# Converting weights with clamp, shift and mask, and two feed-forward chunks in halves, in a fused attention and feed-forward kernel

## The chip, the core and the metric

The kernel runs on one core of a Trainium2 chip. A core has a matrix engine (TensorE, PE in the profile), a vector engine (VectorE, DVE), a scalar engine (ScalarE, ACT), a general engine (GpSimd, POOL) and a queue that starts transfers (SyncE, SP). Each engine works through its own instructions in order and waits for others by semaphores. Matmuls write to PSUM, all else lives in SBUF. The metric is device time in microseconds (us) of one execution.

## What is computed

```python
def _attn_ref(q, k, v, w_phi):                  # q, k, v: 8 x 8 heads x 576 x 64
    def phi(x):
        proj = np.einsum('bhsd,df->bhsf', x, w_phi)                 # 64 -> 128
        proj = proj - np.max(np.abs(proj), axis=-1, keepdims=True)
        return np.concatenate([np.exp(proj), np.exp(-proj)], axis=-1)
    q_p, k_p = (phi(q), phi(k))
    kv = np.einsum('bhsf,bhsd->bhfd', k_p, v)
    z = np.sum(k_p, axis=2)
    num = np.einsum('bhsf,bhfd->bhsd', q_p, kv)
    den = np.einsum('bhsf,bhf->bhs', q_p, z)[..., None] + 1e-06
    return (num / den).astype(np.float32)

def _moe_ref(x, w_in, w_out):                   # x: 4608 x 512, w_in: 512 x 2048
    h = x @ w_in
    sp = np.where(h > 20.0, h, np.log1p(np.exp(np.minimum(h, 20.0))))
    g = h * np.tanh(sp)                         # Mish
    return (g @ w_out).astype(np.float32)       # w_out: 2048 x 512
```

The attention's output, 4608 tokens of 512 features, is the feed-forward's `x`. The attention's inputs are fp32, but `w_in` and `w_out` arrive as fp64; the kernel sees each element as two 32-bit words.

## The kernel before

**Attention.** The keys are cut into 36 key units of 512 columns (two heads). A unit is loaded (`k_load`, tile `kraw`), projected on PE (`k_proj`, `pp_k`, L122), its absolute maxima are taken on DVE (L127) and subtracted (L128), ACT makes two exponentials (`k_exp`), and PE adds keys times values into `kvps` (`k_sum`, L137); DVE copies each finished head pair to `kv` (L182). Values come by `v_load`, with `v` triple-buffered. The 4608 queries go in 18 chunks of 256 tokens with two query units each, (chunk, 0) and (chunk, 1): projection `pp_q`, maxima, subtraction to `e_q`, transposes to `dt` (L200), exponentials (L202), `num` on PE, a division on DVE (L217 to L219), and transposes to `xt`. ACT and DVE then split the result into `xTh` and `xTl`, two parts that together hold its fp32 precision. Queries of one batch need its `kv`, and so 4.5 key units.

**Feed-forward.** Each chunk runs through 16 tiles f of 128 hidden features. `ff_in` is 12 matmuls to `h` (L249, three products of the high and low parts by four weight pieces); `mish` takes two tiles at a time, Mish on ACT (L257) with a table of its own, and `gh` and `gl` as the two parts (L261, L262); `ff_out` is six matmuls of 512 columns (L276) into two `o` accumulators, which stay in PSUM for all 16 tiles of a chunk.

**Weights.** They are 32 pieces of 128 x 512: `in` (i, j), four row blocks i by four column blocks j, and `out` i, 16 row blocks. Tile f of `h` needs `in` (0 to 3, f // 4), and step f of `o` needs `out` f. The order is `in` j=0, then `out` 0-3, `in` j=1, `out` 4-7, `in` j=2, `out` 8-11, `in` j=3, `out` 12-15. `load_weight` fetches one piece (512 KB), `split_weight` (L81 to L101) turns the words into fp32 with a low remainder: DVE takes mantissa and exponent (L88, L89), ACT converts both to floats (L91, L92), DVE adds the low word (L93) and the sign (L94), POOL multiplies (L96), ACT rounds to the high part (L100), POOL subtracts for the low part (L101). The tile `w` shares three buffers with Mish's `u`.

**Order.** Every step is put at a time in a list (`at`), whose unit is one feed-forward tile: tile n of the 288 stands at n. From time -2 on a key and a query unit stand at every eighth unit; ahead of that, seven key units from -18.8 on lie 2.4 apart (`USTART`), the last two with the first two query units. The 32 pieces' conversions are spread evenly from -16.8 to 9, each loaded 3 ahead. The list is emitted in order of time, and the framework's scheduler then moves instructions a little by its own timeline. What stands on an engine is in fixed order.

Of the kernel before, what the change touches and what calls it, by code (L numbers as in the profile page):

```python
# [39 lines left out]
def attention_then_mish(ctx, tc, qT, kT, va, w_phi, w_in, w_out, out):  # L40
    nc = tc.nc

    const = ctx.enter_context(tc.tile_pool(name="const", bufs=1))
# [10 lines left out]
    one = const.tile([P, 1], F32, tag="one", name="one")
    nc.vector.memset(one, 1.0)
    exp_bias = const.tile([P, 1], F32, tag="exp_bias", name="exp_bias")
    nc.vector.memset(exp_bias, -7.0 * 2 ** 30)
# [23 lines left out]
    def split_weight(kind, i, j):  # L81

        nm = f"{kind}_{i}_{j}"
        words = weight[kind, i, j]
# [2 lines left out]
        scale = work.tile([P, 512], U32, tag="half", name=f"scale_{nm}", bufs=NHALF)
        nc.vector.tensor_scalar(w, high, 0xFFFFF, None, op0=ALU.bitwise_and)  # L88
        nc.vector.tensor_scalar(scale, high, 1, 21, op0=ALU.logical_shift_left, op1=ALU.logical_shift_right)  # L89

        nc.scalar.activation(w.bitcast(F32), w, AF.Identity, scale=2.0 ** -20, bias=one)  # L91
# [1 line left out]
        nc.vector.scalar_tensor_tensor(w.bitcast(F32), low, 2.0 ** -52, w.bitcast(F32), op0=ALU.mult, op1=ALU.add)  # L93
        nc.vector.scalar_tensor_tensor(scale, high, 0x80000000, scale, op0=ALU.bitwise_and, op1=ALU.bitwise_or)  # L94
# [1 line left out]
        nc.gpsimd.tensor_tensor(w, w, scale.bitcast(F32), op=ALU.mult)  # L96
# [3 lines left out]
        nc.scalar.copy(hi, w)  # L100
        nc.gpsimd.tensor_sub(lo, w, hi.bitcast(F32))  # L101
# [134 lines left out]

    def ff_in(c, f):
        nonlocal starting
# [24 lines left out]
            g_live[c, 2 * fp + f] = (gh, gl)  # L263

    def ff_out(c, f):
        if f == 0:
            o_live[c] = [ps_o.tile([P, DM], F32, tag="o", name=f"o_{c}_{tt}") for tt in range(2)]
        if f == NFT - 2:
            return
        for tt, ps in enumerate(o_live[c]):  # L270
            cols = slice(tt * P, (tt + 1) * P)
            for i in (f - 1, f) if f == NFT - 1 else (f,):
                gh, gl = g_live[c, i]
                wh, wl = weight["out", i, 0]
                for k, (g, w) in enumerate(((gh, wh), (gh, wl), (gl, wh))):
                    nc.tensor.matmul(ps, g[:, cols], w, start=(i == 0 and k == 0), stop=(i == NFT - 1 and k == 2))  # L276
            if f == NFT - 1:
                o = work.tile([P, DM], F32, tag="half", name=f"osb_{c}_{tt}", bufs=NHALF)
                if c == NCH - 1 and tt:
                    nc.vector.tensor_copy(o, ps)  # L280
                else:
                    nc.scalar.copy(o, ps)
                nc.sync.dma_start(out[c * CH + tt * P:c * CH + (tt + 1) * P, :], o)


    events = []
# [5 lines left out]
    steps = [(n - LEAD, n if n < NK else None, divmod(n - LEAD, 2) if 0 <= n - LEAD < 2 * NCH else None)
             for n in range(LEAD + 2 * NCH)]
    when = {n: 8.0 * n - 18.0 if n >= 2 else 8.0 * 2 - 18.0 - USTART * (2 - n) for n in range(-LEAD, 2 * NCH + 1)}
    for n, key, query in steps:
        t, t1 = when[n], when[n + 1]
# [19 lines left out]
    t0 = when[-LEAD]  # L316
    for i, pc in enumerate(pieces):
        when = t0 + W0 + (W1 - W0 - t0) * i / 31
        at(when - WLOAD, load_weight, *pc)
        at(when, split_weight, *pc)  # L320
# [41 lines left out]
```

## Time and profile before

| what | us |
|---|---|
| median of 3 runs (1248.95 to 1250.86) | 1249.59 |
| the profiled execution | 1249.79 |
| its span in the profile | 1247.8 |
| PE busy in the span | 1174.2 (94%) |
| ACT busy | 616.0 (49%) |
| DVE busy | 499.2 (40%) |
| POOL busy (all of it ahead of 185 us) | 91.0 (7%) |

The span is that of one execution taken by the profiler; the execution's own time is 2.0 longer. The page's columns "busy" count time with an instruction in progress, waiting for a port within an instruction included. A PE share of 94% says nothing by itself on where the other 6% lie, nor at which clock PE ran; the slices and stretches of the prediction do.

### The profile page before, as it was taken

Reading aid. Unit: us, or ns where it says so; the run is one execution under the profiler, and the core shown is the slowest. Engines: PE = TensorE matmul, PEld = TensorE weight load, DVE = VectorE, ACT = ScalarE, POOL = GpSimd, SP = SyncE. Lnnn points to the kernel's source line nnn. Section 1 sums busy time; section 2 is a strip of 40 time slices with the busy share of each in tenths; the row PEclk is TensorE's granted clock in tenths of the full one; section 3 lists DMA queues with packets and bytes.
Section 4 is the critical chain, followed back from the end, with each engine's and each line's share of the span. In section 5 each row is a group of like instructions: output and inputs, shape, how many; then the busy total and the mean of one; then the engine's idle time right before and its main releaser. Section 6 shows DMA issues by size and latency. Waiting matters only on the chain.

```text
span 1247.8 us, 26586 instructions
## 1 busy us (share of the span) xinstructions
PE 1174.2 (94%) x11632; PEld 1050.6 (84%) x11632; DVE 499.2 (40%) x991; ACT 616.0 (49%) x1023; POOL 91.0 (7%) x70
## 2 busy tenths in 40 slices
PE   5436899999999999999999999999999999999998
PEld 4426788888889888888898989888888889999997
DVE  7997783333333333333333333333333332222221
ACT  5544676454545454545445445444444445545421
POOL 3663350000000000000000000000000000000000
PEclk9567889999999999999999999999999999999999
DMA  9811101011111111011111111111011100000000
GB/s 354 329 28 44 34 9 46 19 46 29 46 29 37 38 29 46 18 46 29 46 29 46 29 46 29 35 29 46 29 46 29 35 18 27 1 18 10 10 18 17
DMA packets 25027, 57.67 MB, mean 46 GB/s; under 512 B 2768, under 2 KB 2896, under 8 KB 24912
## 3 DMA queue, kind: packets, MB, share of 16 engines
q1 hardware_dynamic: 24912, 55.98, 13.7%
q8 instruction: 91, 1.49, 0.5%
q14 instruction: 24, 0.20, 0.0%
HBM read 46.53 MB, written 9.44 MB: 45 GB/s over the span
## 4 chain that ended last, share of the span: by engine, by line
PE 89%; DVE 7%; ACT 1%; issue 1%; DMA 0%; POOL 0%; SPq 0%; DVEq 0%; ACTq 0%; POOLq 0%
PE o L276 33%; PE h L249 33%; PE kvps L137 5%; PE pp_q L122 5%; PE num L137 5%; PE pp_k L122 3%; PE dt L200 2%; PE xt L227 1%; DVE scale_in L94 1%; DVE w_in L93 1%; DVE scale_in L89 1%; DVE scale_out L89 1%; DVE w_out L93 1%; DVE m_k L127 1%; DVE w_in L88 1%
## 5 line engine op out<-in xcount | busy, mean ns | idle before, releaser
L249 PE MATMUL h<-xTh,win 128*128 128x256 f32 x2304 | 454.0, 282 | 1.5 <-DVE e_q L128 1.5
L249 PEld LDWEIGHTS h<-xTh,win 128*128 128x128 f32 x2304 | 370.9, 188 | 17.4 <-issue 1.7
L276 PE MATMUL o<-wout,gh 128*128 128x512 f32 x1152 | 380.1, 409 | 2.2 <-DVE kv L182 2.2
L262 DVE TENSOR_TENSOR gl<-u,gh 128x256 fp32r<-128x256 f32 x288 | 118.4, 439 | 548.6 <-ACT gh L261 546.2
L257 ACT ACTIVATE u<-h 128x512 f32<-128x512 f32 x144 | 86.1, 598 | 499.3 <-PE h L249 495.0
L249 PE MATMUL h<-xTl,win 128*128 128x256 f32 x1152 | 324.6, 282 | 0.0
L276 PE MATMUL o<-wout,gl 128*128 128x512 f32 x576 | 228.4, 397 | 0.0
L249 PEld LDWEIGHTS h<-xTl,win 128*128 128x128 f32 x1152 | 216.8, 188 | 12.1
L276 PEld LDWEIGHTS o<-wout,gh 128*128 128x128 f32 x1152 | 197.1, 190 | 34.8 <-DVE kv L182 2.4
L276 PEld LDWEIGHTS o<-wout,gl 128*128 128x128 f32 x576 | 108.9, 189 | 25.9 <-issue 0.2
L261 ACT CAST gh<-u 128x256 fp32r<-128x256 f32 x288 | 110.9, 409 | 38.7 <-PE o L276 19.6
L122 PE MATMUL pp_k<-w_phi,kraw 64*128 64x128 f32 x576 | 64.6, 315 | 32.8 <-issue 16.3
L122 PEld LDWEIGHTS pp_k<-w_phi,kraw 64*128 64x128 f32 x576 | 52.8, 212 | 50.7 <-issue 49.4
L137 PE MATMUL kvps<-v,e_k 128*64 128x66 f32 x2560 | 91.0, 233 | 1.6 <-ACT e_k L166 1.6
L137 PEld LDWEIGHTS kvps<-v,e_k 128*64 128x64 f32 x2560 | 85.1, 146 | 7.4 <-ACT e_k L166 2.3
L257 ACT ACT_TABLE_LOAD x68 | 87.2, 1283 | 1.2
L202 ACT ACTIVATE e_q<-dt 128x512 f32<-128x512 f32 x144 | 78.2, 595 | 17.0 <-PE dt L200 16.5
L202 ACT ACT_TABLE_LOAD x67 | 86.0, 1283 | 1.0
L137 PE MATMUL num<-kv,e_q 128*64 128x66 f32 x2304 | 77.3, 224 | 6.7 <-ACT e_q L202 5.0
L122 PE MATMUL pp_q<-w_phi,qraw 64*128 64x128 f32 x576 | 74.3, 293 | 7.1 <-issue 3.9
L137 PEld LDWEIGHTS num<-kv,e_q 128*64 128x64 f32 x2304 | 73.1, 140 | 8.6 <-ACT e_q L202 5.2
L122 PEld LDWEIGHTS pp_q<-w_phi,qraw 64*128 64x128 f32 x576 | 62.1, 195 | 16.8 <-issue 14.1
(45 smaller groups left out, 809.4 us busy)
## 6 DMA issues: line engine op xcount, KB each, us to landing
v<-va SPq DMA_DIRECT2D x32, 330.0 KB, 3.0
...
```

Of the source, the lines that this page charges most:

```text
L88: nc.vector.tensor_scalar(w, high, 0xFFFFF, None, op0=ALU.bitwise_and)
L89: nc.vector.tensor_scalar(scale, high, 1, 21, op0=ALU.logical_shift_left, op1=ALU.logical_shift_right)
L93: nc.vector.scalar_tensor_tensor(w.bitcast(F32), low, 2.0 ** -52, w.bitcast(F32), op0=ALU.mult, op1=ALU.add)
L122: nc.tensor.matmul(ps[j][:, n], raw[rows, n * P:(n + 1) * P], w_phi2[rows], start=True, stop=True)
L137: nc.tensor.matmul(ps[rows], lhsT[:, rows], rhs[h], start=start, stop=stop, skip_group_check=True)
L200: nc.tensor.transpose(ps[:, n * P:(n + 1) * P], e[:, 0, n * P:(n + 1) * P], ident)
L202: table(nc.scalar.activation(e[:, s, :], ps, AF.Exp, scale=2.0 * s - 1.0))
L249: nc.tensor.matmul(ps, w[:, wcol], x[:, cc % 2, :], start=(n == 0), stop=(n == 11))
L257: table(nc.scalar.activation(u, hv, AF.Mish))
L261: nc.scalar.copy(gh, u[:, f * CH:(f + 1) * CH])
L262: nc.vector.tensor_sub(gl, u[:, f * CH:(f + 1) * CH], gh.bitcast(F32))
L276: nc.tensor.matmul(ps, g[:, cols], w, start=(i == 0 and k == 0), stop=(i == NFT - 1 and k == 2))
```

## The change

**Conversion.** One ACT instruction (Abs) copies the high words, which lie at every second place, to a packed tile. DVE clamps them as floats, shifts them left by 3 under a mask, and puts sign and top bit back; that is the fp32 value. A mask keeps sign and exponent (`t`), and `low * 2^-52 * t` is what the low word adds. ACT rounds to the high part, POOL subtracts and adds. So per piece ACT has two instructions where it had three, DVE five where it had four, and POOL two as before.

**Feed-forward order.** The first two chunks (`NHALVED`) go through tiles 0-7 of chunk 0, 0-7 of chunk 1, 8-15 of chunk 0, 8-15 of chunk 1. The first half's `o` is copied to `part` in SBUF by ACT, and DVE adds it to the second half's.

**Time table.** Five key units lead, then four query units, then four key units (`FIRST_STEPS`); from time 14 on the steps are as before. Conversions stand at `WTIMES` (12 pieces ahead of -2 to 2, the last at 22), loads at a line of their own from -19 on, 0.6 apart. `v` has two buffers where it had three.

```diff
+SMALL, LARGE = 2.0 ** -15, 1.875 * 2.0 ** 16 - 2.0 ** -7
-NRAW, NE, NV, NKV = 4, 6, 3, 10
+NRAW, NE, NV, NKV = 4, 6, 2, 10
+FIRST_STEPS = ((-16.0, 0, None), (-14.0, 1, None), (-12.0, 2, None), (-10.0, 3, None), (-8.0, 4, None), (-6.0, None, 0),
...
-W0, W1 = 2.0, 9.0
+NHALVED = 2
+WL0, WL1 = -19.0, 0.6
+WTIMES = [t0 + (t1 - t0) * i / 4 for t0, t1 in ((-14, -7), (-7, -2), (-2, 2), (2, 6), (6, 10), (10, 14), (14, 18), (18, 22))
+          for i in range(4)]
...
-        nc.vector.tensor_scalar(w, high, 0xFFFFF, None, op0=ALU.bitwise_and)
-        nc.vector.tensor_scalar(scale, high, 1, 21, op0=ALU.logical_shift_left, op1=ALU.logical_shift_right)
-        nc.scalar.activation(w.bitcast(F32), w, AF.Identity, scale=2.0 ** -20, bias=one)
-        nc.scalar.activation(scale, scale, AF.Relu, scale=2.0 ** 23, bias=exp_bias)
-        nc.vector.scalar_tensor_tensor(w.bitcast(F32), low, 2.0 ** -52, w.bitcast(F32), op0=ALU.mult, op1=ALU.add)
-        nc.vector.scalar_tensor_tensor(scale, high, 0x80000000, scale, op0=ALU.bitwise_and, op1=ALU.bitwise_or)
+        nc.scalar.activation(w.bitcast(F32), high.bitcast(F32), AF.Abs)
+        nc.vector.tensor_scalar(w.bitcast(F32), w.bitcast(F32), SMALL, LARGE, op0=ALU.max, op1=ALU.min)
+        nc.vector.tensor_scalar(w, w, 3, 0x3FFFFFF8, op0=ALU.logical_shift_left, op1=ALU.bitwise_and)
+        nc.vector.scalar_tensor_tensor(w, high, 0xC0000000, w, op0=ALU.bitwise_and, op1=ALU.bitwise_or)
+        nc.vector.tensor_scalar(t.bitcast(U32), w, 0xFF800000, None, op0=ALU.bitwise_and)
+        nc.vector.scalar_tensor_tensor(t, low, 2.0 ** -52, t, op0=ALU.mult, op1=ALU.mult)
         w = w.bitcast(F32)
-        nc.gpsimd.tensor_tensor(w, w, scale.bitcast(F32), op=ALU.mult)
         nc.scalar.copy(hi, w)
-        nc.gpsimd.tensor_sub(lo, w, hi.bitcast(F32))
+        nc.gpsimd.tensor_sub(w, w, hi.bitcast(F32))
+        nc.gpsimd.tensor_tensor(lo, w, t, op=ALU.add)
...
+            if f < NFT - 1:
+                part_live[c, tt] = work.tile([P, DM], F32, tag="part", name=f"part_{c}_{tt}", bufs=2 * NHALVED)
+                nc.scalar.copy(part_live[c, tt], ps)
+                continue
+            if parts == 2:
+                nc.vector.tensor_tensor(o, ps, part_live.pop((c, tt)), op=ALU.add)
...
+    tiles = [(c, half * NFT // 2 + f) for half in range(2) for c in range(NHALVED) for f in range(NFT // 2)]
+    tiles += [(c, f) for c in range(NHALVED, NCH) for f in range(NFT)]
     for n in range(total):
-        c, f = divmod(n, NFT)
+        c, f = tiles[n]
```

Two places show how the instructions move. The first is DVE, where the first query unit's subtraction `e0_q_0_0` stands; names carry the piece or unit and end in a buffer number. Before:

```order
L88 TENSOR_SCALAR w_out_8_0_1034<-words_out_8_0_858 128x512
L93 SCALAR_TENSOR_TENSOR w_in_3_2_1011<-words_in_3_2_826,w_in_3_2_1011 128x512
L89 TENSOR_SCALAR scale_out_8_0_1035<-words_out_8_0_858 128x512
L128 TENSOR_TENSOR e0_q_0_0_630<-pp0_q_0_0_620,m0_q_0_0_631 128x512
L93 SCALAR_TENSOR_TENSOR w_out_8_0_1034<-words_out_8_0_858,w_out_8_0_1034 128x512
L128 TENSOR_TENSOR e1_q_0_0_634<-pp1_q_0_0_621,m1_q_0_0_635 128x512
L94 SCALAR_TENSOR_TENSOR scale_out_8_0_1035<-words_out_8_0_858,scale_out_8_0_1035 128x512
```

And now:

```order
L94 TENSOR_SCALAR w_in_3_1_819<-w_in_3_1_819 128x512
L98 SCALAR_TENSOR_TENSOR t_in_2_1_786<-words_in_2_1_202,t_in_2_1_786 128x512
L95 SCALAR_TENSOR_TENSOR w_in_3_1_819<-words_in_3_1_206,w_in_3_1_819 128x512
L97 TENSOR_SCALAR t_in_3_1_820<-w_in_3_1_819 128x512
L98 SCALAR_TENSOR_TENSOR t_in_3_1_820<-words_in_3_1_206,t_in_3_1_820 128x512
L132 TENSOR_TENSOR e0_q_0_0_520<-pp0_q_0_0_510,m0_q_0_0_521 128x512
L132 TENSOR_TENSOR e1_q_0_0_524<-pp1_q_0_0_511,m1_q_0_0_525 128x512
L186 COPY kv_2_424<-kvps_2_339 128x264
L186 COPY kv_3_491<-kvps_3_426 128x264
L131 TENSOR_REDUCE m0_q_0_1_628<-pp0_q_0_1_617 128x4
```

The subtraction stood among pieces `in` (3, 2) and `out` 8, the 20th and 21st; now it stands behind the 12th, `in` (3, 1), and no piece stands behind it until the first feed-forward tiles.

The second place is PE, at the first use of the last column block, `in` (0, 3), by tile 12 of chunk 0. Before, step 7 of chunk 0's `o` and key unit 9 stand ahead of it:

```order
L276 MATMUL o_0_0_1225<-wout_7_0_823,gh1_0_3_1460 128x512 x2
L276 MATMUL o_0_0_1225<-wout_7_0_823,gl1_0_3_1461 128x512
L276 MATMUL o_0_1_1226<-wout_7_0_823,gh1_0_3_1460 128x512 x2
L276 MATMUL o_0_1_1226<-wout_7_0_823,gl1_0_3_1461 128x512
L122 MATMUL pp0_k_9_1678<-w_phi2_83,kraw_9_1571 128x128
...
L249 MATMUL h_0_12_1631<-xTh_0_0_854,win_0_3_1193 128x256
L249 MATMUL h_0_12_1631<-xTl_0_0_855,win_0_3_1193 128x256
```

Now the last first-half step of chunk 1's `o` does:

```order
L283 MATMUL o_1_0_0_1584<-wout_7_0_1059,gh1_1_3_1767 128x512 x2
L283 MATMUL o_1_0_0_1584<-wout_7_0_1059,gl1_1_3_1768 128x512
L283 MATMUL o_1_0_1_1585<-wout_6_0_1006,gh0_1_3_1763 128x512 x2
L283 MATMUL o_1_0_1_1585<-wout_6_0_1006,gl0_1_3_1764 128x512
L283 MATMUL o_1_0_1_1585<-wout_7_0_1059,gh1_1_3_1767 128x512 x2
L283 MATMUL o_1_0_1_1585<-wout_7_0_1059,gl1_1_3_1768 128x512
L253 MATMUL h_0_12_1959<-xTh_0_0_663,win_0_3_1662 128x256
L253 MATMUL h_0_12_1959<-xTl_0_0_664,win_0_3_1662 128x256
```

Tile 12 of chunk 0 was the 13th feed-forward tile on PE and is the 21st; eight tiles of chunk 1 have moved ahead of it.

More of the change, by code (lines that the diff above doesn't have):

```diff
@@ L53, in attention_then_mish @@
     make_identity(nc, ident)
[L54 to L57, printed above, removed]
     w_phi2 = const.tile([P, F], F32, tag="w_phi", name="w_phi2")
@@ L83, in split_weight @@
         nm = f"{kind}_{i}_{j}"
-        words = weight[kind, i, j]
-        low, high = words[:, :, 0], words[:, :, 1]
+        low, high = (weight[kind, i, j][:, :, k] for k in range(2))
         w = moe.tile([P, 512], U32, tag="u", name=f"w_{nm}", bufs=3)
[L87 to L91, printed above, removed]
-        nc.scalar.activation(scale, scale, AF.Relu, scale=2.0 ** 23, bias=exp_bias)
-        nc.vector.scalar_tensor_tensor(w.bitcast(F32), low, 2.0 ** -52, w.bitcast(F32), op0=ALU.mult, op1=ALU.add)
-        nc.vector.scalar_tensor_tensor(scale, high, 0x80000000, scale, op0=ALU.bitwise_and, op1=ALU.bitwise_or)
+        t = work.tile([P, 512], F32, tag="half", name=f"t_{nm}", bufs=NHALF)
+        nc.scalar.activation(w.bitcast(F32), high.bitcast(F32), AF.Abs)
[4 more added lines that the diff above has]
+        nc.vector.scalar_tensor_tensor(t, low, 2.0 ** -52, t, op0=ALU.mult, op1=ALU.mult)
         w = w.bitcast(F32)
-        nc.gpsimd.tensor_tensor(w, w, scale.bitcast(F32), op=ALU.mult)
         parts = slot_tile(f"w{nm}", F32R, f"w{nm}")
@@ L232, in q_out @@
         xT[c, g] = (hi, lo)
-    h_live, g_live, o_live = {}, {}, {}
+    h_live, g_live, o_live, part_live = {}, {}, {}, {}
     def ff_in(c, f):
@@ L265, in ff_out @@
     def ff_out(c, f):
-        if f == 0:
-            o_live[c] = [ps_o.tile([P, DM], F32, tag="o", name=f"o_{c}_{tt}") for tt in range(2)]
-        if f == NFT - 2:
+        parts = 2 if c < NHALVED else 1
+        first, end = f - f % (NFT // parts), f - f % (NFT // parts) + NFT // parts - 1
+        if f == first:
+            o_live[c] = [ps_o.tile([P, DM], F32, tag="o", name=f"o_{c}_{f}_{tt}") for tt in range(2)]
+        if f == end - 1:
             return
@@ L271, in ff_out @@
             cols = slice(tt * P, (tt + 1) * P)
-            for i in (f - 1, f) if f == NFT - 1 else (f,):
+            for i in (f - 1, f) if f == end else (f,):
                 gh, gl = g_live[c, i]
@@ L275, in ff_out @@
                 for k, (g, w) in enumerate(((gh, wh), (gh, wl), (gl, wh))):
[L276 to L283, printed above, removed]
+                    nc.tensor.matmul(ps, g[:, cols], w, start=(i == first and k == 0), stop=(i == end and k == 2))
+            if f < end:
+                continue
+            if f < NFT - 1:
+                part_live[c, tt] = work.tile([P, DM], F32, tag="part", name=f"part_{c}_{tt}", bufs=2 * NHALVED)
+                nc.scalar.copy(part_live[c, tt], ps)
+                continue
+            o = work.tile([P, DM], F32, tag="half", name=f"osb_{c}_{tt}", bufs=NHALF)
+            if parts == 2:
+                nc.vector.tensor_tensor(o, ps, part_live.pop((c, tt)), op=ALU.add)
+            elif c == NCH - 1 and tt:
+                nc.vector.tensor_copy(o, ps)
+            else:
+                nc.scalar.copy(o, ps)
+            nc.sync.dma_start(out[c * CH + tt * P:c * CH + (tt + 1) * P, :], o)
     events = []
@@ L289, in at @@
         events.append((time, len(events), fn, args))
[L292 to L296, printed above, removed]
+    steps = [(time, key, None if q is None else divmod(q, 2)) for time, key, q in FIRST_STEPS]
+    for n in range(4, 2 * NCH):
+        steps.append((8.0 * n - 18.0, n + LEAD if n + LEAD < NK else None, divmod(n, 2)))
+    steps.append((8.0 * 2 * NCH - 18.0, None, None))
+    for (t, key, query), (t1, _, _) in zip(steps, steps[1:]):
         d = t1 - t
@@ L315, in attention_then_mish @@
             at(t1 + GX, q_out, *query)
[L316 to L320, printed above, removed]
+    for i, (pc, time) in enumerate(zip(pieces, WTIMES)):
+        at(WL0 + WL1 * i, load_weight, *pc)
+        at(time, split_weight, *pc)
+    tiles = [(c, half * NFT // 2 + f) for half in range(2) for c in range(NHALVED) for f in range(NFT // 2)]
+    tiles += [(c, f) for c in range(NHALVED, NCH) for f in range(NFT)]
     total = NCH * NFT
     for n in range(total):
-        c, f = divmod(n, NFT)
+        c, f = tiles[n]
         at(n, ff_in, c, f)
```

7 lines of the change are left out of this document (4 added, 3 removed).

## The prediction

> **What bounds the kernel now.** The page's second part comes first: where is TensorE (PE) not full?
>
> ```profile
> span 1247.8 us, 26586 instructions
> ...
> PE   5436899999999999999999999999999999999998
> ...
> DVE  7997783333333333333333333333333332222221
> ...
> PEclk9567889999999999999999999999999999999999
> ```
>
> A digit is 31.2 us. PE is short of work in the first five only; there VectorE (DVE) is the full engine. From about 160 us on PE is at nine tenths or more, at full clock, until the end. So only the start can be shortened. Six stretches show how it ends:
>
> ```profile
> 8.30:106.30 98.00, 43.13 (x488) 38.43 (x488) 96.22 (x124) 56.64 (x92) 62.55 (x44) 0.66 0.56 212
> 106.30:127.70 21.40, 17.33 (x321) 15.97 (x321) 14.64 (x32) 7.54 (x15) 0.00 (x0) 0.87 0.26 69
> 127.70:151.50 23.80, 19.58 (x257) 17.84 (x257) 15.86 (x26) 15.61 (x26) 7.45 (x6) 0.95 0.10 28
> 151.50:166.20 14.70, 14.70 (x47) 11.56 (x48) 13.76 (x23) 8.09 (x13) 7.61 (x6) 0.50 0.07 20
> 166.20:260.80 94.60, 94.50 (x961) 84.45 (x960) 44.02 (x83) 52.13 (x87) 12.74 (x9) 1.00 0.10 28
> 260.80:1247.80 987.00, 982.85 (x9548) 880.57 (x9546) 314.58 (x706) 474.67 (x791) 0.00 (x0) 1.00 0.10 31
> ```
>
> The columns are stretch, length, then busy time (count) of PE, its weight loads, DVE, ScalarE (ACT), GpSimd (POOL), then PE clock, DMA share, GB/s. Until 106.3 us DVE has 96.2 of 98.0 us, and POOL does 44 operations, two per weight piece, so 22 pieces are converted. Then POOL stands still for 21 us (the query chain). At 127.7 us the feed-forward (FF) begins, and 260.8 us is the end of chunk 1's last `h` tile. **Behind that point the PE work is the same before and after** (by the two orders: 256 `h` tiles, 261 `o` tiles, 30 query units), so the new time is the new moment of that point plus 987.0, plus the 2.0 us by which the execution (1249.79) exceeds its span.
>
> Why is DVE so slow per piece?
>
> ```profile
> 69.55 1.26 POOL L96 TENSOR_TENSOR w_out<-w_out,scale_out 128x512 f32<-128x512 f32 x1 [1.56 <-DVE scale_out L94]
> 72.43 1.28 POOL L101 TENSOR_TENSOR wout<-w_out,wout 128x512 fp32r<-128x512 f32 x1 [1.63 <-ACT wout L100]
> ...
> 84.29 0.41 DVE L88 TENSOR_SCALAR w_in<-words_in 128x512 uint32<-128x512 uint32 x1
> 84.63 0.68 DVE L93 SCALAR_TENSOR_TENSOR w_in<-words_in,w_in 128x512 f32<-128x512 uint32 x1
> 84.74 0.72 ACT L91 ACTIVATE w_in<-w_in,one 128x512 f32<-128x512 uint32 x1 [1.28 <-DVE w_in L88]
> 85.23 0.41 DVE L89 TENSOR_SCALAR scale_in<-words_in 128x512 uint32<-128x512 uint32 x1
> ...
> 85.45 1.32 POOL L96 TENSOR_TENSOR w_in<-w_in,scale_in 128x512 f32<-128x512 f32 x1 [1.63 <-DVE w_in L93]
> 85.56 1.75 DVE L93 SCALAR_TENSOR_TENSOR w_in<-words_in,w_in 128x512 f32<-128x512 uint32 x1
> ...
> L128 DVE TENSOR_TENSOR e_k<-pp_k,m_k 128x512 f32<-128x512 f32 x12 | 8.2, 681 | 0.1
> ```
>
> From start to start a `tensor_scalar` takes 0.34 us (84.29 to 84.63) and a two-input operation 0.60 (84.63 to 85.23). The second L93, issued just as a POOL operation starts, lasts 1.75: it ends 0.54 us behind POOL. So DVE operations with SBUF inputs and POOL operations exclude each other. Operations that read PSUM (the L128 group) keep their 0.68 throughout. One piece then costs 2 x 0.34 + 2 x 0.60 + 1.26 + 1.28 = 4.42 us of a shared resource, and 22 pieces 97.2 us: all of the 98.0 us. **The conversion's shared path bounds the start**; the attention's DVE work hides beneath POOL.
>
> **The change, part by part.**
>
> *Conversion.* DVE gets three `tensor_scalar` and two two-input operations, ACT one Abs for two conversions, POOL still two. That is 3 x 0.34 + 2 x 0.60 = 2.22, plus 2.54, so 4.76 us a piece. No row shows a clamp, or an operation in place on packed words. Its bounds are 0.34 (L88, L89: the same kind, 512 words) and 0.60 (two-input); nothing in the trace does 512 words quicker. I take 0.34, the nearest kind, and keep 0.60 for the range. ACT's saving is worth nothing: it is busy 57 of 98 us.
>
> *Fewer pieces ahead of FF.* By the order 12 pieces, five key units and query (0,0)'s maxima stand ahead of `e0_q_0_0` on DVE, where 22 stood. First words at 8.35 us (start of DVE's work in the first stretch), Abs 0.72, 12 x 4.76 = 57.1, less the last piece's POOL (2.54): 63.6. Now the five steps of a piece follow each other and often stand in adjacent rows, so I add 1.4: 65 us.
>
> *The query chain*, then, has no weight work beside it:
>
> ```profile
> 72.77 2.04 PE L122 MATMUL pp_q<-w_phi,qraw 64*128 64x128 f32 x14 [3.04 <-DVE e_k L128]
> 93.83 0.68 DVE L128 TENSOR_TENSOR e_q<-pp_q,m_q 128x512 f32<-128x512 f32 x1
> 94.66 1.09 PE L200 MATMUL dt<-ident,e_q 128*128 128x128 f32 x4 [15.08 <-DVE e_q L128]
> ...
> 103.68 1.08 ACT L202 ACTIVATE e_q<-dt 128x512 f32<-128x512 f32 x2
> ...
> 112.82 1.16 PE L122 MATMUL pp_q<-w_phi,qraw 64*128 64x128 f32 x16
> ...
> 127.65 0.35 PE L249 MATMUL h<-xTh,win 128*128 128x256 f32 x1 [1.48 <-DVE e_q L128]
> ```
>
> Before, `pp_q` of query (0,1) at 112.82 to the first `h` at 127.65 is 14.8 us. Query (0,0)'s `num` rows now stand there, where key 7's stood. Ahead of it come two subtractions (1.3), the copy that frees a PSUM bank for the last 16 `kvps` rows and those rows (an estimate, 1.7), two transposes at half clock (2.2) and `pp_q` at half clock (2.0): 7.2. In all 22 us, so **FF starts at 87 us, where it was 127.7**.
>
> *FF against the other 20 pieces.* The first piece behind the chain (out 4) waits for the first Mish and its table switch. POOL's first work behind FF's start came 7.5 us later before:
>
> ```profile
> 135.15 1.33 POOL L96 TENSOR_TENSOR w_out<-w_out,scale_out 128x512 f32<-128x512 f32 x1 [28.92 <-DVE w_out L93]
> ```
>
> I take 7: 94 us. The next point that can hold PE is chunk 0's tile 12, which needs 16 of those pieces; PE's queue is in order, and nothing passes it. Among them stand 18 `gl` subtractions (SBUF inputs, so they exclude POOL too):
>
> ```profile
> L262 DVE TENSOR_TENSOR gl<-u,gh 128x256 fp32r<-128x256 f32 x10 | 8.9, 909 | 2.7 <-ACT gh L261 2.6
> L93 DVE SCALAR_TENSOR_TENSOR w_out<-words_out,w_out 128x512 f32<-128x512 uint32 x6 | 6.9, 1151 | 7.3 <-ACT w_out L91 7.3
> ...
> L262 DVE TENSOR_TENSOR gl<-u,gh 128x256 fp32r<-128x256 f32 x288 | 118.4, 439 | 548.6 <-ACT gh L261 546.2
> L257 ACT ACT_TABLE_LOAD x68 | 87.2, 1283 | 1.2
> ```
>
> The first two rows are of 128.0 to 184.4 us, the others of the whole run. Packed: 16 x 4.76 + 18 x 0.44 = 84.1. Before, ten pieces and ten `gl` (48.6 packed, less four operations done earlier, 46.7) took 56.4 us; without the first wait of some 6 us for ACT, which my 7 us hold already, that is 1.08 of packed. The first stage ran at 1.00. I take 1.07: 90 us, so **the 28th piece is ready at 184 us**.
>
> Where is PE by then? Its prices at full clock:
>
> ```profile
> 301.00 1.41 PE h L249 x12
> 302.41 1.40 PE o L276 x6
> ...
> 305.23 0.44 PE dt L200 x4
> ...
> 312.69 1.09 PE pp_k L122 x16
> ...
> 315.39 2.49 PE kvps L137 x80
> 317.88 1.87 PE num L137 x64
> 319.76 1.09 PE pp_q L122 x8
> ```
>
> From FF's start to tile 12 the order holds 19 `h` tiles (26.8), 16 `o` tiles (22.4), 3.6 `kvps` units (9.0), 1.1 `num` (2.0), five key and two query projections (5.5 + 4.4), eight transposes (3.5, xT's priced like dt): 73.6. The same prices give 968 us for the last stretch's 985, so I add 2%: 75. PE would be there at 162 and waits until 184. Behind it, to the end of chunk 1: 46 us by the same count. Last, the clock. In the fourth stretch PE was busy for all 14.7 us, yet its granted clock stayed at 0.50, behind the 4.2 us of idle time in the stretch ahead of it; that is 7.3 us lost. I charge it once: 184 + 46 + 7 = 237. **237 + 987 + 2 = 1226 us**, 24 below the profiled execution, which lies 0.2 above the runs' median of 1249.59.
>
> On that clock: the Trainium skill, "TensorE: Matmul & The Clock Gate", "What's actually happening", lets the clock rise after one busy window of about 3.4 us. By that rule the last term would be 1.7 and the sum, an estimate, about 1220. The fourth stretch disagrees (14.7 us busy at 0.50).
>
> *Taken at nothing:* ten more table loads (146 against 136 in ACT's order) of 1.28, since ACT has some 73 us of work in those 97; if ACT led, up to 12.8. Four copies to `part` and four adds on DVE: behind FF's start DVE is half idle (44.0 of 94.6 us); uncovered 2.4. `v` has two buffers, and `v_2` stands on SP behind all 32 weights:
>
> ```profile
> 40.00:50.00 10.00, 0.55 (x16) 0.41 (x12) 10.00 (x11) 3.91 (x6) 7.54 (x6) 0.67 1.02 405
> ...
> v<-va SPq DMA_DIRECT2D x32, 330.0 KB, 3.0
> ```
>
> Some 19 MB go ahead of it, 47 us at 405 GB/s. `kvps_2` stands on PE behind query (0,0)'s projection, whose banks come free only at DVE's tenth piece (8.35 + 10 x 4.76 = 56 us). Uncovered, each of `v_2` to `v_4` costs up to 3 us.
>
> **The rivals.**
>
> *B: conversion keeps up.* If the new DVE operations did not exclude POOL, or other waits were shorter, PE alone would set the pace from 87 us: 75 + 49 = 124, so 211, and 1200 us. For it: the first stage ran with its shared path full, and the in-weights are now wanted later in PE's order. Against it: 84 us packed do not fit into 75. From 94 to 162 us, with the same 1.07, it needs pieces of 3.5 us.
>
> *C: the in-place `tensor_scalar`s run at the two-input price*, 0.60. Then 0.78 more per piece: 9.4 for the first 12, 13.4 for the next 16, together 23, and 1249. For it: no row shows the clamp. Against it: L88 and L89, whose shape and kind are the same. The Trainium skill, "VectorE: DVE Perf Modes", "The perf-mode tier table", gives fp32 `tensor_scalar` in SBUF twice the rate of two-input operations; by it C falls away, and no run here shows the form.
>
> *D: slower, by the clock.* PE is now starved inside FF, not ahead of it. If its clock stays at 0.50 for a share x of the 75 us of work, tile 12 comes at 87 + 75(1 + x); it lies behind the weights from x = 0.29 on, and the end of chunk 1 (49 more) behind the old 260.8 from x = 0.66 on. At x = 0.8 the end is 271, the time 1260. For it: the fourth stretch, half clock with PE full. Against it: the third, 0.95 with PE 82% busy.
>
> **How the numbers follow.** My forecast, that the conversion bounds until the 28th piece, has 0.66 at 1226, and its own range is 1212 (packed at 1.00: 6 less; no clock loss: 7 less) to 1242 (FF 8 later, ACT's loads partly open). B has 0.16 around 1200, C 0.10 around 1249, D 0.08 around 1260. A measurement of this kernel tells some 0.2% (2.5 us) from no change. The range reaches from 1202, which takes in about half of B, to 1250, which takes in C's bound; D and the edges are left out. Faster: 0.65 of the forecast, B, and half of C, 0.86. Same: 0.04. Slower: D and the rest of C, 0.10.
>
> **What would show it.** In the new profile: the first L253 `h` near 87 us (step two wrong if above 100); the last POOL operation of piece 12 near 68 us; the clamp, shift and mask rows at 0.41 when POOL is idle (C if near 0.68); POOL's 28th piece near 184, with PE idle or at half clock ahead of it (B if PE is full from 90 us on); the last `h` of chunk 1 near 237, and 987 us from there to the end. If that last stretch changes, something outside the start moved, and the whole sum is wrong.

## The result, and the profile after

| | time, median of 4 runs (us) | first and last | profiled execution |
|---|---|---|---|
| before, same chip | 1250.22 | 1248.95 to 1252.40 | 1249.79 |
| after | 1229.28 | 1228.85 to 1229.99 | 1228.85, span 1226.9 |

The ratio is 0.9831, 95% interval [0.9814, 0.9848]: the kernel became 1.7% faster, 1229 us where 1226 was forecast.

The page of the changed kernel, its busy tenths (a digit is 30.7 us):

```profile
span 1226.9 us, 26595 instructions
...
PE   4589788999999999999999999999999999999998
...
DVE  7958787333333333333333333333333332222221
...
POOL 3514444000000000000000000000000000000000
PEclk9599988999999999999999999999999999999999
```

PE stands at seven tenths and more from the third digit on (before, from the fifth), but reaches its steady nine only at the eighth: VectorE and POOL now stay busy up to the seventh digit, and there, in the midst of the feed-forward, PE falls back to 7 and 8 tenths. By stretches (columns as in the prediction):

```profile
5.70:68.90 63.20, 32.14 (x437) 29.37 (x436) 60.14 (x88) 26.35 (x44) 34.16 (x24) 0.71 0.84 324
79.70:132.00 52.30, 47.76 (x501) 41.77 (x499) 36.36 (x78) 36.54 (x55) 17.08 (x12) 0.97 0.11 28
132.00:160.00 28.00, 20.36 (x234) 17.43 (x235) 24.85 (x37) 18.11 (x30) 14.73 (x10) 0.92 0.15 44
160.00:181.20 21.20, 20.95 (x173) 18.65 (x172) 17.55 (x31) 14.83 (x26) 8.84 (x6) 0.94 0.10 29
181.20:200.00 18.80, 13.81 (x118) 11.20 (x120) 17.46 (x24) 14.17 (x21) 11.77 (x8) 0.82 0.06 15
200.00:239.90 39.90, 39.90 (x443) 35.97 (x440) 20.22 (x45) 17.63 (x31) 5.23 (x4) 1.00 0.14 40
239.90:1226.90 987.00, 982.78 (x9543) 881.59 (x9542) 315.97 (x707) 473.65 (x789) 0.00 (x0) 1.00 0.10 31
79.70:239.90 160.20, 142.78 (x1462) 125.02 (x1461) 116.43 (x213) 101.29 (x159) 57.64 (x40) 0.95 0.12 33
```

The last stretch is cut at 987.0 us from the end, as it was before, and its busy times are those of before within 2 us. By the matmuls themselves, chunk 1's last `h` tile now ends at 239.6 us, 987.3 us from the end; before it ended at 261.0, 986.8 from the end. So the whole gain lies in front of it. The last row is the stretch from the first `h` matmul to there. Before it was this one:

```profile
127.65:260.80 133.15, 128.83 (x1262) 113.90 (x1263) 73.68 (x130) 75.82 (x125) 27.80 (x20) 0.94 0.10 27
```

So the feed-forward began 48.0 us sooner (79.7 instead of 127.65), and 27.1 of these were given back behind its start: 14.0 as busy time of PE (142.78 against 128.83), 13.1 as idle time of PE (17.4 against 4.3). The busy time is that of 200 matmuls more (1462 against 1262): rows of keys and queries that stood ahead of the first `h` before. At the full-clock prices of the prediction they are some 9 us; the other 5 are longer rows. The moments that the prediction named, in the timeline of the changed kernel (start, length, then what ran):

```profile
6.45 0.43 DVE L93 TENSOR_SCALAR w_in<-w_in 128x512 f32<-128x512 f32 x1 [6.45 <-ACT w_in L92]
...
65.12 1.28 DVE L132 TENSOR_TENSOR e_q<-pp_q,m_q 128x512 f32<-128x512 f32 x2
...
67.63 1.27 POOL L105 TENSOR_TENSOR win<-w_in,t_in 128x512 fp32r<-128x512 f32 x1
...
79.70 0.48 PE L253 MATMUL h<-xTh,win 128*128 128x256 f32 x2
...
92.56 0.43 DVE L93 TENSOR_SCALAR w_out<-w_out 128x512 f32<-128x512 f32 x1 [4.75 <-ACT w_out L92]
...
179.66 0.28 PE L253 MATMUL h<-xTh,win 128*128 128x256 f32 x1
...
181.23 0.39 PE L253 MATMUL h<-xTh,win 128*128 128x256 f32 x1 [0.29 <-ACT win L103]
...
186.47 1.35 POOL L105 TENSOR_TENSOR win<-w_in,t_in 128x512 fp32r<-128x512 f32 x1
...
188.69 0.50 PE L253 MATMUL h<-xTh,win 128*128 128x256 f32 x2
...
239.28 0.28 PE L253 MATMUL h<-xTh,win 128*128 128x256 f32 x1
```

In order: the first clamp, query (0,0)'s subtraction, the end of piece 12 on POOL (68.9), the first `h`, the first step of piece 13, PE at chunk 0's tile 12 (the 241st of the `h` matmuls, 20 tiles of 12 lie ahead), the same tile's third weight piece, the end of the 28th piece on POOL (187.8), the first use of that piece's low part, the end of chunk 1's last `h` tile (239.6).

The prediction had PE wait once, at tile 12. There PE waits 0.5 us in all for weights; it fills the time between that tile's pieces with other matmuls. Where PE waits in fact is shown by the same timeline between 148 and 156 us:

```profile
148.09 1.81 DVE L98 SCALAR_TENSOR_TENSOR t_out<-words_out,t_out 128x512 f32<-128x512 uint32 x1
149.44 1.62 POOL L105 TENSOR_TENSOR wout<-w_out,t_out 128x512 fp32r<-128x512 f32 x1
149.83 1.51 DVE L93 TENSOR_SCALAR w_out<-w_out 128x512 f32<-128x512 f32 x1
151.02 1.46 POOL L104 TENSOR_TENSOR w_out<-w_out,wout 128x512 f32<-128x512 f32 x1
151.38 1.38 DVE L94 TENSOR_SCALAR w_out<-w_out 128x512 uint32<-128x512 uint32 x1
151.52 0.45 PE L141 MATMUL kvps<-v,e_k 128*64 128x66 f32 x8
152.56 1.32 POOL L105 TENSOR_TENSOR wout<-w_out,t_out 128x512 fp32r<-128x512 f32 x1
152.79 1.63 DVE L95 SCALAR_TENSOR_TENSOR w_out<-words_out,w_out 128x512 uint32<-128x512 uint32 x1
...
155.81 0.43 DVE L186 COPY kv<-kvps 128x264 f32<-128x264 f32 x1
...
156.29 2.07 PE L126 MATMUL pp_q<-w_phi,qraw 64*128 64x128 f32 x8 [4.32 <-DVE kv L186]
```

PE finishes a key unit's values at 151.97 (151.52 + 0.45). The copy that frees their PSUM bank takes 0.43 us, but stands behind the conversion steps in VectorE's queue, seven from 148.09 on, and four of these last 1.4 to 1.8 us in place of 0.42 or 0.69: each started beside a POOL operation and ended just behind it. PE stands still for 4.3 us. So here it is the conversion that PE waits for, but by way of attention work queued behind it, not by way of a weight. The Trainium skill, "SBUF — State Buffer", "Who interferes with whom", says that such a VectorE operation and a GpSimd one that reads SBUF block each other whole, and that whichever issues first wins; these rows agree.

The other long waits ahead of tile 12 (6.3 us in five) are for a key unit's exponentials. ScalarE's rows ahead of the longest of them, and PE's:

```profile
127.02 1.24 ACT L92 ACTIVATE w_in<-words_in 128x512 f32<-128x512 f32 x2 [0.20 <-DVE gl L266]
128.27 1.28 ACT L261 ACT_TABLE_LOAD   x1
129.57 0.60 ACT L261 ACTIVATE u<-h 128x512 f32<-128x512 f32 x1
130.18 1.28 ACT L169 ACT_TABLE_LOAD   x1
131.48 0.63 ACT L169 ACTIVATE e_k<-e_k 128x512 f32<-128x512 f32 x1
...
132.61 0.62 ACT L170 ACTIVATE e_k<-e_k 128x512 f32<-128x512 f32 x1
...
133.29 1.62 PE L141 MATMUL kvps<-v,e_k 128*64 128x66 f32 x48 [2.73 <-ACT e_k L170]
```

Two table loads and a Mish stand directly ahead of the exponentials, and two copies of the conversion (L92) ahead of those.

### The profile page after: what moved, and what is told of

Its sections match the earlier page's. It is cut to its first block, busy times and chain, and to the rows that moved or that the text cites. A ratio compares the mean times of both kernels' runs of the same rounds, so it can differ in the third digit from the quotient of the medians.

```text
span 1226.9 us, 26595 instructions
## 1 busy us (share of the span) xinstructions
PE 1170.1 (95%) x11632; PEld 1047.4 (85%) x11632; DVE 500.1 (41%) x1025; ACT 607.3 (49%) x1001; POOL 92.5 (8%) x70
## 4 chain that ended last, share of the span: by engine, by line
PE 84%; DVE 6%; issue 5%; ACT 3%; POOL 2%; DMA 0%; SPq 0%; POOLq 0%; DVEq 0%; ACTq 0%
PE h L253 31%; PE o L283 31%; PE kvps L141 5%; PE num L141 5%; PE pp_q L126 5%; PE pp_k L126 3%; PE dt L204 2%; PE xt L231 1%; DVE w_in L95 1%; DVE w_out L95 1%; POOL w_in L104 1%; POOL w_out L104 1%; POOL wout L105 1%; DVE w_out L93 1%; POOL win L105 1%
## 5 line engine op out<-in xcount | busy, mean ns | idle before, releaser
L253 PEld LDWEIGHTS h<-xTh,win 128*128 128x128 f32 x2304 | 373.2, 189 | 19.3 <-ACT u L261 2.2
L266 DVE TENSOR_TENSOR gl<-u,gh 128x256 fp32r<-128x256 f32 x288 | 113.7, 423 | 522.1 <-ACT gh L265 520.0
L141 PE MATMUL kvps<-v,e_k 128*64 128x66 f32 x2560 | 90.6, 233 | 12.2 <-ACT e_k L170 7.7
L141 PEld LDWEIGHTS kvps<-v,e_k 128*64 128x64 f32 x2560 | 84.7, 146 | 18.8 <-ACT e_k L170 9.3
L126 PEld LDWEIGHTS pp_k<-w_phi,kraw 64*128 64x128 f32 x576 | 46.4, 205 | 43.3 <-issue 41.8
L126 PE MATMUL pp_k<-w_phi,kraw 64*128 64x128 f32 x576 | 57.4, 309 | 26.2 <-issue 14.6
```

The costliest lines, as they stand in the source:

```text
L126: nc.tensor.matmul(ps[j][:, n], raw[rows, n * P:(n + 1) * P], w_phi2[rows], start=True, stop=True)
L141: nc.tensor.matmul(ps[rows], lhsT[:, rows], rhs[h], start=start, stop=stop, skip_group_check=True)
L253: nc.tensor.matmul(ps, w[:, wcol], x[:, cc % 2, :], start=(n == 0), stop=(n == 11))
L266: nc.vector.tensor_sub(gl, u[:, f * CH:(f + 1) * CH], gh.bitcast(F32))
```

## The experiments

All twelve kernels were timed beside before; the changed kernel stands at 0.9831. A difference to it is (ratio - 0.9831) x 1249.6 us, and is good to some 3 us. The moments are from POOL's and PE's timelines of one profiled execution each. `e7`, `e9` and `e11` change nothing that runs ahead of the first `h`, and theirs comes 1.1 to 1.9 us later than the changed kernel's, so differences of such moments under some 2 us mean nothing.

| run | time (us) | ratio to before | piece 12 ends | first `h` | 28th piece ends |
|---|---|---|---|---|---|
| before | 1249.2 to 1250.2 | 1 | 66.3 | 127.65 | 167.7 |
| after | 1229.28 | 0.9831 [0.9814, 0.9848] | 68.9 | 79.70 | 187.8 |
| e1_old_conv | 1229.29 | 0.9837 [0.9817, 0.9858] | 60.8 | 78.64 | 182.5 |
| e2_new_conv | 1258.88 | 1.0072 [1.0052, 1.0092] | 72.9 | 124.96 | 175.0 |
| e3_nhalved0 | 1266.82 | 1.0138 [1.0121, 1.0155] | 69.6 | 94.84 | 182.0 |
| e5_dense | 1267.16 | 1.0141 [1.0124, 1.0159] | 69.4 | 95.44 | 182.8 |
| e6_nhalved0_wide | 1251.28 | 1.0021 [1.0007, 1.0035] | 70.6 | 87.05 | 191.8 |
| e10_halves_e6times | 1250.64 | 1.0005 [0.9996, 1.0014] | 69.8 | 87.08 | 190.1 |
| e7_no_dve | 1214.44 | 0.9714 [0.9697, 0.9731] | 69.0 | 80.77 | 165.5 |
| e9_two_more_later | 1243.25 | 0.9949 [0.9929, 0.9968] | 69.9 | 81.55 | 197.9 |
| e8_two_more_first12 | 1241.18 | 0.9928 [0.9911, 0.9944] | 78.9 | 90.62 | 198.7 |
| e11_abs_twice_later | 1234.48 | 0.9874 [0.9860, 0.9889] | 69.3 | 81.05 | 193.1 |
| e4_pool_to_dve | 1220.38 | 0.9763 [0.9744, 0.9781] | | 75.15 | |
| e12_one_pool_then_dve | 1223.48 | 0.9787 [0.9772, 0.9802] | 64.6 | 77.70 | |

The theory is the prediction's: VectorE's and POOL's summed time per piece sets the pace, and the 28th piece the end. The rivals: that the pace is the chain VectorE, ScalarE, POOL; that PE or ScalarE leads; that halves do, or don't, matter.

### The conversion exchanged alone

`e1_old_conv` is the changed kernel with the `split_weight` of before; `e2_new_conv` is the kernel of before with the new one.

```diff
 e1: -        nc.scalar.activation(w.bitcast(F32), high.bitcast(F32), AF.Abs)
 ...
 e1: +        nc.vector.tensor_scalar(w, high, 0xFFFFF, None, op0=ALU.bitwise_and)
 e1: +        nc.vector.tensor_scalar(scale, high, 1, 21, op0=ALU.logical_shift_left, op1=ALU.logical_shift_right)
 ...
```

> The changed schedule (five key units first, halves, 12 pieces then the rest) with the conversion of before (two operations more on ScalarE, one fewer on VectorE). If the price per piece is the DVE/POOL one of the prediction (4.42 us instead of 4.76 us), the end of chunk 1 comes up to 28 x 0.34 = 9.5 us sooner than with the new conversion: about 1220 us. Rival: what sets a piece's pace is the chain DVE to ACT to POOL; the old conversion has two more ACT steps and passes to POOL once before the cast and once behind it, so a piece is no cheaper: 1229 us or more (up to 1240).

> The schedule of before with the new conversion alone. If a piece costs 0.34 us more on DVE beside POOL, 22 pieces ahead of the query chain and 6 behind make it 7 to 9.5 us slower than before: 1257 to 1260 us. Rival (chain rather than price): the new conversion's two POOL operations stand together at the end of a piece, which changes little or saves: 1245 to 1252 us.

`e2` is 9.0 us slower than before, the size that the price gave, but by another way. Its 22nd piece ends at 122.5 us (106.2 before), yet its first `h` comes 2.7 us sooner: query (0,0)'s subtraction stands behind 15 finished pieces (at 88.27 us) where it stood behind 18 (93.83). It loses its time in the feed-forward, where PE's timeline has one great wait for a Mish:

```profile
185.65 0.58 PE L251 MATMUL h<-xTh,win 128*128 128x256 f32 x1 [11.72 <-ACT u L259]
```

`e1` is a miss: piece 12 comes 8.1 us and the 28th 5.3 us sooner, and the time is the same (0.7 us more, within 3). Neither point sets the end by itself: PE comes to tile 12 at 185.6, 3 us behind the 28th piece. In front, query (0,0)'s subtraction comes only 2.4 us sooner (62.76), and the first `h` 1.1. The last key unit's subtractions, which free the banks of the query's projection, run at 55.78 and 57.58 there (49.44 and 52.38 in the changed kernel), among more conversion steps. Behind the first `h`, this is its stretch:

```profile
78.64:240.50 161.86, 143.02 (x1460) 125.31 (x1459) 113.57 (x189) 109.20 (x175) 54.26 (x40) 0.93 0.11 32
```

VectorE's 116.4 us became 113.6, and ScalarE's 101.3 became 109.2. That suggested that ScalarE's time has a price too; see `e11` below.

### Halves, and the due times

`e3_nhalved0` sets `NHALVED = 0`, which needs earlier due times (tile 12 of chunk 0 stands at 12 without halves and at 20 with them), here for the tenth piece and all behind it; `e5_dense` has the halves with these times. `e6_nhalved0_wide` and `e10_halves_e6times` are the same pair with times as late as whole chunks allow.

```diff
 after:  (-2, 2), (2, 6), (6, 10), (10, 14), (14, 18), (18, 22)
 e3, e5:  (-2, 0), (0, 2), (2, 4), (4, 6), (6, 8), (8, 10)
 e6, e10: (-2, 1), (1, 4), (4, 7.5), (7.5, 9.5), (9.5, 11.7), (11.7, 16)
 e3, e6:  NHALVED = 0
```

Each pair is the start and the end of four pieces, whose last stands at three quarters of it: the 32nd piece at 21 in the changed kernel, at 9.5 in the first pair and at 14.9 in the second.

> The changed kernel without halves (chunk 0 takes all 16 tiles, then chunk 1), its last 20 pieces asked for in the shorter stretch from -2 to 10 since tile 12 of chunk 0 needs the 28th. By the prediction PE then has 79 us of work ahead of the 28th piece's first use where it has 107 us with halves, so up to 28 us more remain behind the 28th piece (184 to 188 us): end of chunk 1 near 265 us, about 1255 us; if the denser pieces come 10 us sooner, 1245 us. Rival: the halves buy nothing because conversion isn't waited for at tile 12: 1229 us, within 3 us.

> The control of the run without halves: the changed kernel with halves, and its last 20 pieces asked for in the same shorter stretch (-2 to 10 instead of -2 to 22). If the 28th piece's moment is set by the conversion's own pace, it stays near 187 us and the time within 3 us of 1229 us; if the spread of the due times holds the pieces back, the 28th piece comes up to 10 us sooner, and the time falls to 1220 us; if denser pieces get in the way of the feed-forward's own ScalarE and VectorE work, it is slower, up to 1238 us.

> The changed kernel without halves, with its last 20 pieces asked for as late as whole chunks allow (third weight column group by 7.5 to 8, fourth by 12, the end by 16; instead of 10, 18 and 22). If the halves' use is that they let the conversion be spread over more feed-forward tiles, this lies between the run with the dense times (1267 us) and the changed kernel (1229 us): about 1250 us. If it is near 1267 us, the spreading needs the halves entirely; if within 4 us of 1229 us, the halves do nothing and only the spread counts.

> The control of the run without halves and middle times (1251 us): with halves, and the same due times (to 16 rather than 22). If the halves' whole use is that they allow later due times, this is within 3 us of 1251 us, as the dense pair was (1267 and 1267 us). If halves also spare PE a wait for the third and fourth column groups, it lies well under, 1235 to 1245 us.

Whole chunks cost 38 and 24 us, which looks like the halves' worth. The controls take it back: with halves and the same times, 1267.2 against 1266.8, and 1250.6 against 1251.3. `e5` is slower than any of its expectations had it (1238 at the most). **At equal due times the halves bring nothing clear of the noise; what counts is how late the later pieces are asked for, and the halves are what makes the latest of these times possible.** Earlier due times hardly make the pieces earlier: the 28th ends 5 to 6 us sooner than in the changed kernel in `e3` and `e5`, and 2 to 4 us later in `e6` and `e10`. They put pieces ahead of other work: ahead of the query chain (first `h` 7.4 to 15.7 us later), and on ScalarE's queue ahead of the Mish that frees the `h` bank. PE's timeline of `e5`, and ScalarE's ahead of the second wait:

```profile
169.10 0.58 PE L253 MATMUL h<-xTh,win 128*128 128x256 f32 x1 [5.92 <-ACT u L261]
...
188.68 0.58 PE L253 MATMUL h<-xTh,win 128*128 128x256 f32 x1 [10.29 <-ACT u L261]
```

```profile
186.10 0.62 ACT L103 CAST wout<-w_out 128x512 fp32r<-128x512 f32 x1 [2.57 <-DVE t_out L98]
186.73 1.28 ACT L261 ACT_TABLE_LOAD   x1
188.03 0.60 ACT L261 ACTIVATE u<-h 128x512 f32<-128x512 f32 x1
```

ScalarE itself stands idle for 2.57 us there: its queue is at a cast that waits for VectorE's conversion step, and the Mish stands behind that cast. In all, waits for `u` hold PE for 24.1 us between 90 and 205 us (24.9 in `e3`, 24.6 in `e10`); in the changed kernel for 2.0. `e6` loses its time elsewhere: 6.6 us for `u`, 8.7 for `gh` and 5.6 for the weights of `h`. That last wait is the one that halves take away, and `e10` loses as much to the Mish.

Together with `e1` and `e2` this tells where the 21 us come from. The new conversion changes nothing in the new order and costs 9 us in the old one, and halves change nothing at equal times. So the gain is the order's: 12 pieces ahead of the first query in place of some 20, and the others asked for late. The new order of the first key and query units, of the loads and of `v`'s buffers came along with it; no run takes these apart.

### VectorE's time taken away and added

`e7_no_dve` leaves the five VectorE steps out from the 13th piece on (POOL's last step then reads `w` in place of `t`, and the values of these weights are not the reference's); `e9_two_more_later` repeats the mask twice there; `e8_two_more_first12` repeats it in the first 12 pieces.

```diff
 e7: +        if pieces.index((kind, i, j)) < 12:
 ...
 e9: +        for _ in range(2 if pieces.index((kind, i, j)) >= 12 else 0):
 e9: +            nc.vector.tensor_scalar(t.bitcast(U32), w, 0xFF800000, None, op0=ALU.bitwise_and)
 e8: the same with < 12
```

> From the 13th piece on the five VectorE steps of a piece are left out (the values of these pieces are wrong; ScalarE's and POOL's steps stay). If conversion on DVE beside POOL sets the pace of the stretch from 86 to 188 us (the prediction's 28th piece), this stretch shrinks to PE's own work: FF starts at 86 us as before, PE-bound end of chunk 1 at about 210 us, 1200 us in all. If PE is held by ScalarE's queue or its own work, at most 5 us are gained: 1224 us or more. In between, the gain of 29 us at most is shared in proportion.

> From the 13th piece on VectorE masks the words twice more (the same values again), 2 x (0.34 to 0.46) us for each of 16 pieces up to the 28th. If the 28th piece's moment, set by DVE's and POOL's summed time, sets the end of chunk 1, it is 11 to 15 us slower: 1240 to 1244 us. If DVE's time in this stretch isn't what PE waits for: within 3 us of 1229 us.

> VectorE masks twice more in each of the first 12 pieces alone: 24 steps of 0.31 to 0.49 us (from the run that had 40 such steps later). If the first stage's DVE and POOL sum sets the start of the feed-forward and that start sets the end, both come 7 to 11 us later: first h tile at 87 to 91 us, 1236 to 1240 us. Rival: in the run with the old conversion the 12th piece ended 8 us sooner and the first h only 1 us, so the query chain has slack of its own against the conversion; then at most 3 us: 1229 to 1232 us.

`e9` is 14.7 us slower and `e8` 12.1: both stretches pass VectorE's time on to the end. In `e8`, 24 steps put piece 12 off by 10.0 us, 0.42 each, and the first `h` by 10.9; VectorE is full there (60.1 of 63.2 us in the changed kernel). In `e9`, 32 steps put the 28th piece off by 10.0 us, 0.31 each, 1.9 of them already in the first `h`. The prediction's price of 0.34 lies between. In `e9` PE does wait at tile 12 for its weights, 5.4 us, as the prediction had it. In this later stretch VectorE is not full, and the runs do not tell whether the fuller queue or the longer chain of each piece costs the time. This also answers for `e1`'s front: when the conversion there is slower, the first `h` follows at once; when it is faster, something else is next. Without the steps (`e7`) the 28th piece comes 22.3 us sooner, but only 14.6 are gained. The stretches of `e9` and `e7`, one after the other:

```profile
81.55:253.40 171.85, 146.55 (x1462) 126.75 (x1460) 135.95 (x253) 101.53 (x159) 57.69 (x40) 0.94 0.10 30
```

```profile
80.77:225.40 144.63, 135.75 (x1462) 120.48 (x1461) 57.58 (x113) 99.70 (x159) 46.36 (x40) 0.98 0.12 36
```

In `e7` PE is busy for 135.8 of 144.6 us: then PE is nearly the bound, and 1214 us is about what this order can reach with the conversion's VectorE steps gone from this stretch. POOL's time falls with them (46.4 us in place of 57.6), so `e7` is not VectorE's share alone.

### ScalarE's time

`e11_abs_twice_later` takes the absolute value a second time from the 13th piece on.

```diff
+        if pieces.index((kind, i, j)) >= 12: nc.scalar.activation(w.bitcast(F32), w.bitcast(F32), AF.Abs)
```

> From the 13th piece on ScalarE takes the absolute value a second time (0.60 to 0.67 us, 20 times, values unchanged); VectorE's and POOL's work is the same. If ScalarE's queue is a price beside VectorE's in the stretch from 86 to 200 us, the time rises by 0.6 us for each of 16 to 20 pieces, 10 to 12 us, or half of it where ScalarE had room: 1234 to 1241 us; that would explain why the old conversion (ScalarE two steps more, VectorE less) gained nothing here. If VectorE's and POOL's sum alone is what counts: within 3 us of 1229 us.

```profile
81.05:245.10 164.05, 146.61 (x1462) 127.14 (x1461) 123.32 (x213) 112.29 (x179) 56.18 (x40) 0.94 0.11 32
```

5.4 us slower for 11.0 us more on ScalarE (112.29 against 101.29), about half; 3.9 of the 5.4 lie in this stretch, the others in a later first `h`, which the edit does not touch. ScalarE, busy 63% of this stretch, has a price too. Its queue is in order, and the casts and Mishes that PE waits for stand behind the conversion's; but the step also lengthens the chain of each piece, and the run does not tell the two apart. By `e9`, 19.5 us more on VectorE cost 11.7 in the stretch, 0.6 each. With these two rates the old conversion (`e1`: 2.9 us less on VectorE, 7.9 more on ScalarE) comes to -1.7 + 0.35 x 7.9 = +1.1 us in the stretch, 0.35 being `e11`'s 3.9 us of stretch by 11.0; 1.7 were measured. That is a fit from single profiles, and its result is smaller than their spread; the runs show only that both engines' time counts.

### POOL's steps moved to VectorE

`e4_pool_to_dve` gives both POOL steps to VectorE; `e12_one_pool_then_dve` gives it both from the 13th piece on, and leaves one to POOL ahead of that.

```diff
-        nc.gpsimd.tensor_sub(w, w, hi.bitcast(F32))
-        nc.gpsimd.tensor_tensor(lo, w, t, op=ALU.add)
+        nc.vector.tensor_sub(w, w, hi.bitcast(F32))
 e4:  +        nc.vector.tensor_tensor(lo, w, t, op=ALU.add)
 e12: +        (nc.gpsimd if pieces.index((kind, i, j)) < 12 else nc.vector).tensor_tensor(lo, w, t, op=ALU.add)
```

> Both of POOL's steps of a piece done by VectorE instead. Theory of the prediction (POOL's time is exclusive of DVE's, 4.76 us a piece): DVE alone would need about 0.34 x 3 + 0.60 x 4 = 3.4 us a piece plus nothing of POOL, 1.3 us less, so the 12 pieces of the first stage end 10 to 16 us sooner than 68.9 us and the time falls by 10 to 18 us: 1211 to 1219 us. Rival: DVE's steps before a piece's cast and the in-order queue set the pace; DVE now also has to wait for ScalarE's cast in the middle of a piece, and other work behind it waits too: 1229 us or slower (up to 1245 us).

> For the first 12 pieces VectorE takes the subtraction and POOL keeps the last addition; from the 13th on VectorE does both. With both on VectorE everywhere (1220 us), the 20 + 2 + 2 PSUM reads of the key and query units, 16 us, are added to DVE's 3.4 us a piece in the first stage, where they lay beside POOL before. With one POOL step a piece they have 15 us of POOL to lie beside again: 12 x (3 x 0.34 + 3 x 0.60 + 1.27) = 49 us instead of 12 x 3.42 + 16 = 57 us, so up to 8 us less than 1220 us: 1212 us. If the order's waits (VectorE for the cast in the middle of a piece, PE for the values) eat it, 1220 us; if POOL's step blocks VectorE more than it hides, 1224 us.

`e4` is the fastest kernel here: 1220.4 us, 0.9763 of before, 8.5 us below the changed kernel. The pages' lines of busy time, of after and of `e4`:

```profile
PE 1170.1 (95%) x11632; PEld 1047.4 (85%) x11632; DVE 500.1 (41%) x1025; ACT 607.3 (49%) x1001; POOL 92.5 (8%) x70
```

```profile
PE 1165.9 (96%) x11632; PEld 1043.3 (86%) x11632; DVE 499.7 (41%) x1089; ACT 608.1 (50%) x1001; POOL 0.7 (0%) x6
```

VectorE does 64 operations more, 0.69 us each, 44 us, and is busy for no longer: that time it had spent blocked by POOL. Yet the gain is at the low end of what was expected, and in the first stage it is 3.2 us (`e_q` at 61.90 instead of 65.12) where the price gave 16. The PSUM reads of the key units and of the first query unit, 22 of them at 0.60, had lain beside POOL and now add up: 5.76 + 0.72 + 12 x 3.42 + 22 x 0.60 = 60.7. PE also waits for a load, in the timeline of `e4`:

```profile
38.01 4.16 SPq L82 DMA_DIRECT2D words_out<-w_out  x4
...
44.45 0.33 SPq L161 DMA_DIRECT2D v<-va  x1
...
53.62 7.47 PE L141 MATMUL kvps<-v,e_k 128*64 128x66 f32 x160 [5.82 <-DMA v<-va]
```

The third `v` is issued behind all 32 weight loads, the last of which is first touched by ScalarE at 190.9 us. That wait is what the prediction took at nothing for the change. It opens once the conversion is quicker, but here it costs nothing that shows: these matmuls end at 61.1, VectorE has no wait of its own ahead of the subtraction at 61.90, and the copies that PE needs next stand behind that subtraction on VectorE (63.10). Loading `v` sooner was not tried. `e12` was to get the cover back and missed: 1223.5 us, no better than `e4`. Its `e_q` came at 63.17, where 6.5 + 49 = 55.6 had been hoped for: six of POOL's twelve steps hold up a VectorE step with SBUF inputs, which then lasts 1.4 to 1.8 us.

## Why the prediction was right, and where it was not

- **FF starts at 87 us.** Near, 2.6 us too late: the first `h` matmuls come at 79.7 amid the query chain, one tile's worth, and the other tiles from 84.4 on. The query's subtraction came at 65.12 where 65 was forecast, by luck: two errors within it cancelled. The first words came 2.6 us sooner than 8.35 us (the first clamp ran at 6.45, not 9.07), and the pieces ran slower: (65.12 - 5.76 - 0.72 + 2.54) / 12 = 5.1 us each, where 12 x 4.76 and the 1.4 make 4.9. The chain from there was 19.3 us where 22 was forecast. `e8` shows that the stage's time does pass to the end.
- **The conversion's price of 0.34.** The row at 6.45 settles rival C: a clamp in place takes 0.43 us, as the shift behind it does, and not 0.68. From start to start it is 0.46 where the next row needs its result, 0.34 otherwise.
- **28th piece at 184 us.** 187.8: the 16 pieces took 95.3 us from 92.56, 1.13 of packed instead of 1.07.
- **PE at tile 12 at 162 us, waiting there until 184.** This step failed. PE came to tile 12 at 179.7 and waited there 0.5 us for weights. From 84.4 us to there PE's rows hold the 19 `h` and 16 `o` tiles that were counted; it took 95.3 us for that work, and the forecast 75. Of the 20 more, 12.2 are idle time in many small waits, for exponentials and a copy that stand behind conversion, table loads and Mishes; up to 5 are lowered clock (granted 0.97, 0.92 and 0.94 in the three stretches behind 79.7); some 3 stay unexplained. So the forecast put into one wait for a weight what PE lost ahead of that point in several others. `e1` shows the difference: a 28th piece 5.3 us sooner bought nothing. `e7` and `e9` bear the larger claim out, that VectorE's and POOL's time leads there.
- **The end of chunk 1 at 237 us.** 239.6, and in part by luck. The forecast had 22 us of waiting and 7 of lowered clock in all; measured were 17.4 us of idle time from the first `h` on, some 8 of lowered clock and as much again that is not broken down, with a start 2.6 us sooner. Nothing in the forecast made these sums agree.
- **7 us for the clock, charged once.** Near in size, wrong in place: the granted clock is 0.95 over the 160.2 us from the first `h` on, 8 us lost at the most, but only 3.4 of them lie behind tile 12 (0.82 in 18.8 us from 181.2). The rest is ahead of it, where the forecast had none.
- **75 us of PE work ahead of the 28th piece.** The count holds, but not the use made of it here: without halves 28 us of it go behind the piece, which made 28 us of loss in what was expected of `e3`. The controls show that halves alone bring nothing; the late due times do. The due times were no term of the forecast.
- **Table loads, partial sums and `v` at nothing.** For `v` the runs agree. For the others they do not quite: one copy to `part` holds PE for 1.3 us, and the ten more table loads (26 ahead of that point instead of 16) stand in the queue that PE waits for, as at 130.18. No run takes them out, so their price is open; ScalarE was not as free as was assumed, 11 us more of it cost 5.
- **The rest.** 987.3 us behind chunk 1 in place of 987.0. Rival B (1200) needed PE full from the start; it stood idle for 17.4 us, and even without VectorE's steps (`e7`) the time is 1214. Rival D did not come: the stretches ahead of 181.2 ran at 0.92 and more.
